# Attention and two feed-forward layers on one core: token blocks of 504 in place of 512, the first two of 472 and 504 in place of 384 and 512

## The chip, the cores and the metric

The kernel runs on one core of a Trainium2 chip. The metric is the device time of one execution in microseconds (us). The profile names the engines: PE is TensorE's matmul, PEld its weight loads, DVE is VectorE, ACT is ScalarE, POOL is GpSimd and SP is SyncE, which issues nearly all DMAs here.

## The reference

What is computed, for 6016 tokens of 256 channels in fp32:

```
qn = q / (norm(q over tokens) + 1e-6);  kn likewise          # q, k: 6016 x 256
a  = softmax(kn.T @ qn / tau)                                # 256 x 256
x  = v @ a                                                   # 6016 x 256
xn = x / rms(x over channels) * rms_g
y  = (silu(xn @ w_gate) * (xn @ w_val)) @ w_out              # d_ff 1536
h  = y @ w_in;  out = (h - tanh(h)) @ w_out2                 # d_ff 2048
```

The first layer's norm is per token; everything after the attention matrix `a` is a chain of matrix products over the tokens.

## The kernel before

Channels lie on the 128 partitions (two halves of 128) and tokens along the free axis, in blocks of up to 512, the width of one fp32 bank of PSUM. A product of 128 x 128 weights with n tokens is made as three fp32r matmuls of n columns each (`prod`, L440 to L453: high by high, low by high, high by low parts), so all weights and operands are split into a high part (a copy on ACT, `hi_of`) and a low part (a subtraction on DVE, `lo_of`). Every matmul has a weight load of its own. A few small or early products are plain fp32 matmuls (`matmul`, L455): the attention scores, `x` of the first two blocks, and the two matmuls of a norm. Each of those stands as two instructions in the trace.

The tokens are cut into twelve blocks, six pairs. Before, they are 384 and 512 for the first pair and 512 for the ten others. The stages are:

- The attention scores, then `x` of blocks 0 and 1 in fp32 (`x_full`), their norms by matmul (`x_post`: `ms` is the mean of squares, `narm`, `nary` and `nart` are the small tiles of the reciprocal root on DVE, `r` spreads it over 128 partitions), and meanwhile `x` of blocks 2 and 3 in three parts (`x_products`).
- The first layer for blocks 0 and 1 with ordinary products (`gate_block`): for each of 12 slices f of the hidden width 4 products (gate and value, two halves of channels) and 2 into the output sums `acc`, for each block: 72 products, so 216 matmuls of the block's width.
- The first layer for pairs 1 to 5 in the form of Strassen and Winograd (`unit`, `first_unit`), in which 7 products stand for 8 over the two blocks of a pair: 132 products a pair. The names in it are X, T, Y, Z with g for gate and v for value, and the operands B11, T1 to T4, B21, B22. Beside it run `x` and the norms of the next pair (`x_thread`): 7 products for each of pairs 2 to 5, and 8 for pair 1.
- The second layer for all six pairs in the same form (`second_unit`): 120 products a pair in 8 units of 7 products and 8 `acc` products. Its first pair takes the tokens of blocks 0 and 1 as two halves of equal width, 448 before.

No engine's order is written out by hand. The code builds a graph of operations (`Graph`), and a planner simulates the engines with cost formulas (`act_cost`, `dve_cost`, n/2.4 + 13.7 ns for a matmul) and emits each engine's instructions in the order found. `LAG1` is the distance, in the planner's time, at which the `acc` products of pairs 1 to 5 are ranked behind the other products of TensorE.

Of the kernel before, what the change touches and what calls it, by code (L numbers as in the profile page):

```python
# [16 lines left out]
P = 128  # L17
# [284 lines left out]
ROUNDS = 6  # L302
FIRST_PIECES, LAST_PIECES = [[1, 1, 2], [2, 2], [2, 2]], [2, 1]
# [3 lines left out]
LAG0, LAG1, LAG2 = 4100.0, 10000.0, 4800.0  # L307
# [4 lines left out]
def attn_moe_kernel(  # L312
# [621 lines left out]
    def x_post(b, xs, ms_tag, r_tag):  # L934

        n = blocks[b][1]
        NG = n // P
        T = {}

        def square(c):  # L940
            T[f"sq{c}"] = sq_tile(f"sq{c}_{b}")
            activation(T[f"sq{c}"][:, :n], xs[c][:, :n], AF.Square, n)

        def gain(c):
            T[f"xg{c}"] = ox(f"x{c}_{b}")
            activation(T[f"xg{c}"][:, :n], xs[c][:, :n], AF.Copy, n, scale=g_t[:, c:c + 1])

        def ms(key=None):
            sq = T["sq0"][:, :n]
            tt("add", sq, sq, T["sq1"][:, :n], n)  # L950
            T["o"] = bank(ms_tag, f"ms{b}")
            for t in range(NG):
                matmul(T["o"][:, 2 * t:2 * t + 2], T["sq0"][:, t * P:(t + 1) * P], mean32, P,
                       True, True, key=key)

        def rs():
            m, y, t = (narrow(x, f"b{b}") for x in "myt")
# [51 lines left out]
    def x_thread(p, take, out):  # L1009


        B = []
# [4 lines left out]
        def split_v(t):  # L1017
            raw = v_raw.pop(b0 + t)
            vh, vl = (new(wpool, f"gv{4 + t}{x}", f"v{x}{b0 + t}", V2, F32R) for x in "hl")
            for kk in range(KC):  # L1020
                g.op("ACT", act_cost(BLK), lambda kk=kk: nc.scalar.activation(
                    out=vh.t[:, kk], in_=raw.t[:, kk], func=AF.Copy), [raw], [vh.part(kk)])
            for kk in range(KC):
                dve(lambda kk=kk: nc.vector.tensor_sub(
                    out=vl.t[:, kk], in0=raw.t[:, kk], in1=f32(vh.t[:, kk])), BLK, 2,
                    [raw, vh.part(kk)], [vl.part(kk)])
            split[t] = vh, vl

        def x_out(t, c, o):
            sqs[t].append(sq_tile(f"sq{b0 + t}_{c}"))  # L1030
            activation(sqs[t][c], o, AF.Square, BLK)
            B.append(ox(f"x{b0 + t}_{c}g"))
            activation(B[-1], o, AF.Copy, BLK, scale=g_t[:, c:c + 1])

        def x_products(t):
            for c in range(KC):
                o = take(f"x{b0 + t}_{c}", c)
                for kk in range(KC):
                    vh, vl = split[t]
                    prod(o, a_hl[kk][c], tuple(  # L1040
                        x.view(lambda a, kk=kk: a[:, kk], kk) for x in (vh, vl)), BLK, kk == 0)
                x_out(t, c, o)

        def v_forms():
# [33 lines left out]
            tt("sub", t2, b21, t2, BLK)  # L1078
            tt("sub", b12, b22, b12, BLK)
# [4 lines left out]
        def x_unit():  # L1084
# [4 lines left out]
            def x_to(t, c):  # L1089
                def f(o, m5=None):  # L1090
                    sqs[t][c] = sq_tile(f"sq{b0 + t}_{c}")
                    x = B[KC * t + c] = ox(f"x{b0 + t}_{c}g")
                    if m5 is not None:
                        add(x, o, m5, BLK)
                    elif (t, c) == (0, 1):
                        copy(x, o, BLK)
                    else:
                        activation(sqs[t][c], o, AF.Square, BLK)
                        copy(x, o, BLK)
                        return  # L1100
                    activation(sqs[t][c], x, AF.Square, BLK)
# [13 lines left out]
        def turn_blocks(e, across):  # L1115
            dve(lambda: nc.vector.transpose(out=across.t, in_=e.t), BLK, 2, [e], [across])
# [71 lines left out]
        yield from operands(B, BLK, out)
# [293 lines left out]
    for p in range(1, NP):  # L1482
# [8 lines left out]
        A = Accumulate(out1_weight, NF1, [BLK, BLK], to_y(p), LAG1,  # L1491
                       rr if p + 1 < NP else sq_tile)
        for i in range(NU1):
# [3 lines left out]
            first_unit(i, x, BLK, A, between)  # L1497
# [60 lines left out]
```

## Time and profile before

| | |
|---|---|
| median of 3 runs | 1109.0 us (1108.97 to 1109.12) |
| profiled execution, its own time | 1108.96 us |
| its span in the trace | 1107.2 us |
| busy share: PE, PEld, DVE, ACT | 99%, 83%, 77%, 63% |
| granted clock of TensorE | 1.0 in every slice (2.4 GHz) |

The span runs from the first instruction to the last in the trace, and 1.8 us of the execution's time lie outside it. Matmuls overlap in the trace, since the end of one is modelled some 160 ns behind the start of the next; what one costs is the distance from its start to the start of the next, called its pitch below.

### The profile page before, as it was taken

The numbers are of one execution on the slowest core, as the hardware profiler recorded it, in microseconds if no ns is written. First come the engines' busy times: TensorE is split into PE (matmuls) and PEld (weight loads), VectorE is DVE, ScalarE is ACT, GpSimd is POOL, SyncE is SP. The second block draws the span as 40 slices with busy tenths as digits, with TensorE's granted clock in tenths as the row PEclk, the third lists the DMA queues.
The fourth block names the chain that finished last, engine by engine and source line by source line (L and its number), as shares of the span: only waits on it lengthen the run. The fifth ranks groups of instructions, "written<-read, shape, count | busy, mean of one in ns | idle before, by whom it ended". The sixth has DMA issues, their size and how long they took to land.

```text
span 1107.2 us, 14156 instructions
## 1 busy us (share of the span) xinstructions
PE 1101.4 (99%) x4944; PEld 921.4 (83%) x4944; DVE 852.2 (77%) x1473; ACT 696.0 (63%) x1223; POOL 0.7 (0%) x6
## 2 busy tenths in 40 slices
PE   9999999999999999999999999999999999999998
PEld 8798988888888888888888899888888888888886
DVE  6999897887788788778766967768668668667664
ACT  7776466666566556646566766657656656656664
POOL 0000000000000000000000000000000000000000
PEclk9999999999999999999999999999999999999999
DMA  9952121114212211311322201101101101100101
GB/s 352 388 196 96 58 72 58 39 38 143 77 39 76 68 58 46 122 58 54 120 81 66 89 1 29 44 1 38 39 1 39 38 1 29 39 1 1 39 1 38
DMA packets 41480, 76.75 MB, mean 69 GB/s; under 512 B 5313, under 2 KB 10945, under 8 KB 41409
## 3 DMA queue, kind: packets, MB, share of 16 engines
q1 hardware_dynamic: 40976, 75.47, 20.4%
q8 instruction: 38, 0.62, 0.2%
q10 hardware_dynamic: 432, 0.39, 0.1%
q14 instruction: 34, 0.27, 0.1%
HBM read 54.00 MB, written 21.78 MB: 68 GB/s over the span
## 4 chain that ended last, share of the span: by engine, by line
PE 98%; DVE 1%; DMA 0%; ACT 0%; SPq 0%; issue 0%; DVEq 0%; ACTq 0%
PE acc L451 40%; PE Yh L451 9%; PE Xh L451 6%; PE Yv L451 6%; PE Yg L451 5%; PE Xg L451 4%; PE Xv L451 4%; PE S L459 4%; PE Zh L451 3%; PE Th L451 3%; PE g L451 3%; PE v L451 3%; PE Zv L451 2%; PE Tg L451 2%; PE Zg L451 2%; PE Tv L451 2%
## 5 line engine op out<-in xcount | busy, mean ns | idle before, releaser
L432 DVE TENSOR_TENSOR ulc<-wc,uc 128x512 fp32r<-128x512 f32 (+1 forms) x192 | 130.2, 679 | 83.7 <-ACT uc L413 81.4
L413 ACT ACTIVATE uc<-wc 128x512 fp32r<-128x512 f32 (+1 forms) x192 | 119.3, 623 | 99.7 <-PE acc L451 86.9
L413 ACT ACTIVATE uc<-tc 128x512 fp32r<-128x512 f32 x120 | 73.3, 627 | 86.5 <-DVE tc L428 82.9
L432 DVE TENSOR_TENSOR ulc<-tc,uc 128x512 fp32r<-128x512 f32 x120 | 79.4, 683 | 0.7 <-ACT uc L413 0.4
L428 DVE TENSOR_TENSOR Zv<-Yv,m5v 128x512 f32<-128x512 f32 x30 | 20.9, 698 | 42.8 <-PE Yv L451 40.7
L413 ACT ACTIVATE wc<-Xh 128x512 f32<-128x512 f32 (+1 forms) x48 | 28.2, 588 | 30.5 <-PE Xh L451 30.5
L428 DVE TENSOR_TENSOR wc<-Xh,wc 128x512 f32<-128x512 f32 (+1 forms) x48 | 32.6, 678 | 19.1 <-ACT wc L413 19.0
L428 DVE TENSOR_TENSOR Zh<-Yh,m5h 128x512 f32<-128x512 f32 (+1 forms) x48 | 33.0, 687 | 16.9 <-ACT m5h L413 14.8
L459 PE MATMUL S<-q,k 128*128 128x256 f32 x188 | 42.2, 384 | 0.5 <-DMA k<-k_in 0.5
L459 PEld LDWEIGHTS S<-q,k 128*128 128x128 f32 x188 | 35.8, 193 | 5.6 <-DMA q<-q_in 0.9
L428 DVE TENSOR_TENSOR wc<-Yh,wc 128x512 f32<-128x512 f32 (+1 forms) x48 | 32.6, 679 | 9.4 <-ACT wc L413 9.3
L413 ACT ACTIVATE wc<-Yh 128x512 f32<-128x512 f32 (+1 forms) x48 | 28.1, 586 | 14.8 <-PE Yh L451 14.8
L428 DVE TENSOR_TENSOR acc<-acc,sq 128x512 f32<-128x512 f32 (+1 forms) x46 | 29.5, 678 | 8.4 <-ACT sq L413 7.7
L413 ACT ACTIVATE m5h<-Th 128x512 f32<-128x512 f32 (+1 forms) x48 | 28.2, 588 | 11.3 <-PE Th L451 11.3
L413 ACT ACTIVATE Yh<-Xh 128x512 f32<-128x512 f32 (+1 forms) x48 | 27.6, 575 | 11.6 <-PE Xh L451 10.4
L428 DVE TENSOR_TENSOR wc<-s,wc 128x512 f32<-128x512 f32 (+1 forms) x48 | 32.3, 674 | 0.8 <-ACT wc L413 0.8
L413 ACT ACTIVATE r<-acc 128x512 f32<-128x512 f32 (+3 forms) x49 | 27.1, 579 | 9.1 <-PE acc L451 8.6
L428 DVE TENSOR_TENSOR wc<-Zh,wc 128x512 f32<-128x512 f32 (+1 forms) x48 | 32.3, 673 | 0.7 <-ACT wc L413 0.7
L428 DVE TENSOR_TENSOR s<-Yh,m5h 128x512 f32<-128x512 f32 (+1 forms) x48 | 32.5, 677 | 0.1
L413 ACT ACTIVATE tc<-Xg 128x512 f32<-128x512 f32 x30 | 17.9, 596 | 22.9 <-PE Xg L451 22.8
L451 PE MATMUL acc<-ulc,w12h 128*128 128x512 f32 x80 | 31.2, 390 | 0.0
L451 PE MATMUL acc<-uc,w12l 128*128 128x512 f32 x80 | 31.2, 390 | 0.0
(984 smaller groups left out, 3489.3 us busy)
## 6 DMA issues: line engine op xcount, KB each, us to landing
vraw<-vT_in SPq DMA_DIRECT2D x11, 512.0 KB, 4.3
y<-r SPq DMA_DIRECT2D x22, 256.0 KB, 2.0
y<-y SPq DMA_DIRECT2D x20, 256.0 KB, 2.6
outT<-r SPq DMA_DIRECT2D x19, 256.0 KB, 2.1
q<-q_in SPq DMA_DIRECT2D x8, 512.0 KB, 9.5
k<-k_in SPq DMA_DIRECT2D x8, 512.0 KB, 9.3
raw<-w_in_in SPq DMA_DIRECT2D x8, 512.0 KB, 4.3
l<-y SPq DMA_DIRECT2D x16, 256.0 KB, 2.9
```

The costliest lines, as they stand in the source:

```text
L413: nc.scalar.activation(out=ap(out), in_=ap(in_), func=func, **{x: ap(a) for x, a in kw.items()})
L428: return dve(lambda: f(out=ap(out), in0=ap(a), in1=ap(b)), n, 2, [a, b], [out])
L432: lambda: nc.vector.tensor_sub(out=ap(out), in0=ap(in_), in1=f32(ap(hi))), n, 2,
L451: nc.tensor.matmul(o, ap(a), ap(b), start=start and i == 0, stop=i == 2, skip_group_check=True)
L459: lambda: nc.tensor.matmul(ap(out), ap(a), ap(b), start=start, stop=stop, **kw),
```

## The change

A constant `SIZE = 504` takes the place of the block width 512 in the token split, with REST = 6016 mod 1008 = 976. Blocks are then 472 and 504 for the first pair and 504 for the ten others, and the two halves of the first pair in the second layer are 488 wide in place of 448. Tiles keep their 512 columns, and operations take the first 504 of them. 504, 472 and 488 are no multiples of 128 or 32, so the norms handle a rest: in `x_post` the last group of 128 tokens starts at n - 128 and overlaps the one before it (block 0 has four groups in place of three); in `x_thread` the turning of 32 x 32 blocks is a piece of 480 columns and one of 32 that overlaps it, and the load of the norms is one of 480 columns and one of 24. `LAG1` goes from 10000 to 11500.

```diff
+SIZE = 504
-LAG0, LAG1, LAG2 = 4100.0, 10000.0, 4800.0
+LAG0, LAG1, LAG2 = 4100.0, 11500.0, 4800.0
...
-    REST = N % (2 * BLK) or 2 * BLK
-    blocks = [(0, REST - min(BLK, REST)), (REST - min(BLK, REST), min(BLK, REST))]
-    blocks += [(t, BLK) for t in range(REST, N, BLK)]
+    REST = N % (2 * SIZE) or 2 * SIZE
+    blocks = [(0, REST - min(SIZE, REST)), (REST - min(SIZE, REST), min(SIZE, REST))]
+    blocks += [(t, SIZE) for t in range(REST, N, SIZE)]
...
-        NG = n // P
+        starts = [t * P for t in range(n // P)] + ([n - P] if n % P else [])
+        NG = len(starts)
...
-            for t in range(NG):
-                matmul(T["o"][:, 2 * t:2 * t + 2], T["sq0"][:, t * P:(t + 1) * P], mean32, P,
+            for t, at in enumerate(starts):
+                matmul(T["o"][:, 2 * t:2 * t + 2], T["sq0"][:, at:at + P], mean32, P,
                        True, True, key=key)
...
         def turn_blocks(e, across):
-            dve(lambda: nc.vector.transpose(out=across.t, in_=e.t), BLK, 2, [e], [across])
+            whole = n // G * G
+            cols = [(0, 0, whole)] + ([(whole, n - G, G)] if n % G else [])
+            for to, at, size in cols:
+                dve(lambda to=to, at=at, size=size: nc.vector.transpose(
+                    out=across.t[:, to:to + size], in_=ap(e)[:, at:at + size]), size, 2, [e], [across.part(to)])
+            across.part().w = [w for to, _, _ in cols for w in across.part(to).w]
...
-            dma(rs[t], back.view(lambda a, t=t: a[t:t + 1, :].to_broadcast([P, BLK])), BLK * P * 4,
-                [back], [rs[t]])
+            whole = n // G * G
+            cols = [(0, 0, whole)] + ([(whole, whole + G - n % G, n % G)] if n % G else [])
+            for to, at, size in cols:
+                dma(rs[t].view(lambda a, to=to, size=size: a[:, to:to + size], to),
+                    back.view(lambda a, t=t, at=at, size=size:
+                              a[t:t + 1, at:at + size].to_broadcast([P, size])), size * P * 4,
+                    [back], [rs[t].part(to)])
...
-        n = REST // 2 if p == 0 else BLK
+        n = REST // 2 if p == 0 else SIZE
...
-        A = Accumulate(out1_weight, NF1, [BLK, BLK], to_y(p), LAG1,
+        A = Accumulate(out1_weight, NF1, [SIZE, SIZE], to_y(p), LAG1,
```

The remaining lines of the diff put n or SIZE where BLK stood. Since the planner sees other costs, the order of instructions moves. The second layer's order on TensorE stays as it was but for the widths; the first layer's and the start's do not. Lines of the changed kernel are one higher than before (L459 becomes L460).

On TensorE at the start, around `x_full` (vraw are the values v, a the attention matrix, vh and vl the parts of v of block 2, ms the mean of squares of block 0), before:

```order
L459 MATMUL x_1_513<-vraw_371,a_486 128x512
L459 MATMUL x_0_492<-vraw_367,a_518 128x384
L459 MATMUL x_1_499<-vraw_367,a_518 128x384
L459 MATMUL x_0_505<-vraw_371,a_518 128x512
L459 MATMUL x_1_513<-vraw_371,a_518 128x512
L451 MATMUL x_0_552<-vh_468,ah_490 128x512
L451 MATMUL x_0_552<-vh_468,al_501 128x512
L451 MATMUL x_0_552<-vl_476,ah_490 128x512
L459 MATMUL ms_561<-mean_81,sq_0_540 128x2 x3
```

and in the changed kernel:

```order
L460 MATMUL x_1_514<-vraw_371,a_486 128x504
L452 MATMUL x_0_528<-vh_468,ah_490 128x504
L452 MATMUL x_0_528<-vh_468,al_499 128x504
L452 MATMUL x_0_528<-vl_476,ah_490 128x504
L460 MATMUL x_0_492<-vraw_367,a_524 128x472
L460 MATMUL x_1_501<-vraw_367,a_524 128x472
L460 MATMUL x_0_508<-vraw_371,a_524 128x504
L460 MATMUL x_1_514<-vraw_371,a_524 128x504
L452 MATMUL x_0_528<-vh_468,ah_538 128x504
L452 MATMUL x_0_528<-vh_468,al_543 128x504
L452 MATMUL x_0_528<-vl_476,ah_538 128x504
L460 MATMUL ms_570<-mean_81,sq_0_541 128x2 x4
```

Three matmuls of block 2 moved ahead of the second half of `x_full`. Between `ms` and the spreading matmul `r` of block 0 there are then 9 of these matmuls, where there were 12.

On DVE a little later, the reciprocal root of block 0's norm, for which `r` waits (it begins with narmb from ms and ends with the last naryb; w10, gv1 and a are other work), before, from its third instruction on:

```order
L428 TENSOR_TENSOR a_518<-a_518,a_486 128x128
L472 SCALAR_TENSOR_TENSOR nartb_588<-naryb_579,narmb_574 128x6
L428 TENSOR_TENSOR a_486<-a_518 128x128
L475 TENSOR_TENSOR nartb_588<-nartb_588,naryb_579 128x6
L476 SCALAR_TENSOR_TENSOR nartb_588<-nartb_588 128x6
L632 TENSOR_TENSOR w10l<-w10y,w10h 128x512
L479 SCALAR_TENSOR_TENSOR naryb_579<-nartb_588,naryb_579 128x6
L482 SCALAR_TENSOR_TENSOR nartb_588<-naryb_579,narmb_574 128x6
L958 TENSOR_SCALAR narmb_610<-ms_594 128x8
L485 TENSOR_TENSOR nartb_588<-nartb_588,naryb_579 128x6
L558 TENSOR_SCALAR gv1y<-gv1y 128x512
L488 SCALAR_TENSOR_TENSOR naryb_579<-nartb_588,naryb_579 128x6
```

and in the changed kernel, the whole of it:

```order
L960 TENSOR_SCALAR narmb_586<-ms_570 128x8
L470 TENSOR_SCALAR naryb_588<-narmb_586 128x8
L473 SCALAR_TENSOR_TENSOR nartb_592<-naryb_588,narmb_586 128x8
L476 TENSOR_TENSOR nartb_592<-nartb_592,naryb_588 128x8
L477 SCALAR_TENSOR_TENSOR nartb_592<-nartb_592 128x8
L480 SCALAR_TENSOR_TENSOR naryb_588<-nartb_592,naryb_588 128x8
L559 TENSOR_SCALAR gv1y<-gv1y 128x512
L483 SCALAR_TENSOR_TENSOR nartb_592<-naryb_588,narmb_586 128x8
L559 TENSOR_SCALAR gv1y<-gv1y 128x512
L486 TENSOR_TENSOR nartb_592<-nartb_592,naryb_588 128x8
L960 TENSOR_SCALAR narmb_614<-ms_594 128x8
L489 SCALAR_TENSOR_TENSOR naryb_588<-nartb_592,naryb_588 128x8
```

The three operations on `a` and the subtraction for w10 no longer stand inside this chain; one operation on gv1 more does.

On TensorE in the first layer, in the last unit of pair 2, around its gate products (uc and ulc are the parts of a finished slice of the hidden width), before:

```order
L451 MATMUL Tg_3188<-T1h,sh_1987 128x512
L451 MATMUL Tg_3188<-T1h,sl_2057 128x512
L451 MATMUL Tg_3188<-T1l,sh_1987 128x512
L451 MATMUL acc_2653<-uc_3158,w12h 128x512
L451 MATMUL acc_2653<-uc_3158,w12l 128x512
L451 MATMUL acc_2653<-ulc_3166,w12h 128x512
L451 MATMUL Yg_3186<-T2h,sh_1987 128x512
L451 MATMUL Yg_3186<-T2h,sl_2057 128x512
L451 MATMUL Yg_3186<-T2l,sh_1987 128x512
L451 MATMUL Xg_3162<-B21h,gv5h 128x512
L451 MATMUL Xg_3162<-B21h,gv5l 128x512
L451 MATMUL Xg_3162<-B21l,gv5h 128x512
```

and in the changed kernel:

```order
L452 MATMUL Yg_3210<-T2h,sh_1864 128x504
L452 MATMUL Yg_3210<-T2h,sl_1967 128x504
L452 MATMUL Yg_3210<-T2l,sh_1864 128x504
L452 MATMUL Xg_3182<-B21h,gv5h 128x504
L452 MATMUL Xg_3182<-B21h,gv5l 128x504
L452 MATMUL Xg_3182<-B21l,gv5h 128x504
L452 MATMUL acc_2690<-uc_3178,w12h 128x504
L452 MATMUL acc_2690<-uc_3178,w12l 128x504
L452 MATMUL acc_2690<-ulc_3186,w12h 128x504
```

The first `acc` product of the slices with the weights w12 moved from ahead of Yg's product with T2 to behind Xg's with B21, two products later.

## Rows read from the trace of the kernel before

**Rows 1.** The page's first part: span; busy time, share and instructions of each engine.

```profile
span 1107.2 us, 14156 instructions
PE 1101.4 (99%) x4944; PEld 921.4 (83%) x4944; DVE 852.2 (77%) x1473; ACT 696.0 (63%) x1223; POOL 0.7 (0%) x6
```

**Rows 2.** The chain that ended last, by engine.

```profile
PE 98%; DVE 1%; DMA 0%; ACT 0%; SPq 0%; issue 0%; DVEq 0%; ACTq 0%
```

**Rows 3.** What PE waited for: total us, times, longest us.

```profile
PE nrm L459 <- DVE mean L506: 1.1, 1, 1.1
PE S L459 <- DMA k<-k_in: 0.5, 1, 0.5
PE Yv L451 <- DVE Zv L428: 0.2, 1, 0.2
```

**Rows 4.** Busy time by stretch: from:to, length, each engine's busy us (count), clock, DMA.

```profile
50.00:75.00 25.00, 24.88 (x127) 20.71 (x126) 24.27 (x66) 23.25 (x46) 0.00 (x0) 1.00 0.68 236
75.00:100.00 25.00, 25.00 (x126) 22.61 (x126) 24.84 (x40) 14.65 (x25) 0.00 (x0) 1.00 0.42 147
142.87:613.74 470.87, 470.65 (x2068) 387.04 (x2068) 374.18 (x667) 290.79 (x517) 0.00 (x0) 1.00 0.23 72
651.54:660.84 9.30, 9.30 (x46) 8.45 (x45) 6.50 (x12) 5.38 (x11) 0.00 (x0) 1.00 0.00 0
708.50:718.70 10.20, 10.20 (x46) 8.45 (x45) 6.72 (x11) 5.91 (x11) 0.00 (x0) 1.00 0.00 0
```

**Rows 5.** Timeline, PE, first layer of blocks 0 and 1: start us, us, instruction.

```profile
99.32 0.39 PE L451 MATMUL g<-xh,gv2h 128*128 128x512 f32 x1
...
105.03 0.33 PE L451 MATMUL acc<-u,w11h 128*128 128x384 f32 x1
...
106.59 0.39 PE L451 MATMUL g<-xh,gv2h 128*128 128x512 f32 x1
```

**Rows 6.** Timeline, PE, second layer, pair 0: first matmuls of two units that follow.

```profile
651.55 0.37 PE L451 MATMUL Xh<-B11h,l24h 128*128 128x448 f32 x1
...
660.85 0.37 PE L451 MATMUL Xh<-B11h,l25h 128*128 128x448 f32 x1
```

**Rows 7.** The same in pair 1.

```profile
708.52 0.39 PE L451 MATMUL Xh<-B11h,l22h 128*128 128x512 f32 x1
...
718.72 0.39 PE L451 MATMUL Xh<-B11h,l23h 128*128 128x512 f32 x1
```

**Rows 8.** Timeline, PE, the start: `x_full` and what follows it.

```profile
48.03 6.18 PE L459 MATMUL x<-vraw,a 128*128 128x384 f32 x16
...
54.27 0.40 PE L451 MATMUL x<-vh,al 128*128 128x512 f32 x1
```

**Rows 9.** Timeline, PE, norm matmuls of block 1 (ms) and block 0 (r), and their followers.

```profile
56.80 0.95 PE L459 MATMUL ms<-mean,sq 128*128 128x2 f32 x8
57.60 0.49 PE L451 MATMUL x<-vh,ah 128*128 128x512 f32 x1
...
59.09 0.90 PE L459 MATMUL r<-ident,naryb 128*128 128x128 f32 x6
59.74 0.48 PE L451 MATMUL x<-vh,ah 128*128 128x512 f32 x1
```

**Rows 10.** Timeline, DVE and PEld, reciprocal root of block 0's norm, first and last.

```profile
55.82 0.16 DVE L958 TENSOR_SCALAR narmb<-ms 128x6 f32<-128x6 f32 x1
...
58.84 0.16 DVE L488 SCALAR_TENSOR_TENSOR naryb<-nartb,naryb 128x6 f32<-128x6 f32 x1
...
59.05 0.30 PEld L459 LDWEIGHTS r<-ident,naryb 128*128 128x128 f32 x2 [0.23 <-DVE naryb L488]
```

**Rows 11.** DVE groups and DMA issues of the later norms: count, busy us, mean ns; KB, us.

```profile
L1116 DVE STREAM_TRANSPOSE across<-sq 128x512 f32<-128x512 f32 x10 | 6.8, 694 | 0.0
rs<-back SPq DMA_DIRECT2D x10, 256.0 KB, 3.6
```

**Rows 12.** Timeline, PE, last matmul.

```profile
1102.84 0.39 PE L451 MATMUL acc<-ulc,l27h 128*128 128x512 f32 x1
```

More of the change, by code (lines that the diff above doesn't have):

```diff
@@ L964, in spread @@
             T["y"] = bank(r_tag, f"r{b}")
-            for t in range(NG):
-                matmul(T["y"][:, t * P:(t + 1) * P],
+            for t, at in enumerate(starts):
+                matmul(T["y"][:, at:at + P],
                        T["yn"].view(lambda a, t=t: a[:, 2 * t:2 * t + 1].to_broadcast([P, P])),
@@ L1020, in split_v @@
             for kk in range(KC):
-                g.op("ACT", act_cost(BLK), lambda kk=kk: nc.scalar.activation(
-                    out=vh.t[:, kk], in_=raw.t[:, kk], func=AF.Copy), [raw], [vh.part(kk)])
+                g.op("ACT", act_cost(n), lambda kk=kk: nc.scalar.activation(
+                    out=vh.t[:, kk, :n], in_=raw.t[:, kk, :n], func=AF.Copy), [raw], [vh.part(kk)])
             for kk in range(KC):
                 dve(lambda kk=kk: nc.vector.tensor_sub(
-                    out=vl.t[:, kk], in0=raw.t[:, kk], in1=f32(vh.t[:, kk])), BLK, 2,
+                    out=vl.t[:, kk, :n], in0=raw.t[:, kk, :n], in1=f32(vh.t[:, kk, :n])), n, 2,
                     [raw, vh.part(kk)], [vl.part(kk)])
@@ L1176, in x_thread @@
             rs.append(sq_tile(f"rs{p}_{t}"))
-            dma(rs[t], back.view(lambda a, t=t: a[t:t + 1, :].to_broadcast([P, BLK])), BLK * P * 4,
-                [back], [rs[t]])
+            whole = n // G * G
[5 more added lines that the diff above has]
+                    [back], [rs[t].part(to)])
+            rs[t].part().w = [w for to, _, _ in cols for w in rs[t].part(to).w]
         for t in range(2):
             for c in range(KC):
-                x = B[KC * t + c]
+                x, r = B[KC * t + c][:, :n], rs[t][:, :n]
                 if p == 1:
-                    tt("mul", x, x, rs[t], BLK)
+                    tt("mul", x, x, r, n)
                 else:
-                    dve(lambda x=x, r=rs[t], c=c: nc.vector.scalar_tensor_tensor(
+                    dve(lambda x=x, r=r, c=c: nc.vector.scalar_tensor_tensor(
                         out=ap(x), in0=ap(x), scalar=ap(g_t[:, c:c + 1]), in1=ap(r), op0=ALU.mult,
-                        op1=ALU.mult), BLK, 2, [x, rs[t], g_t], [x])
-        yield from operands(B, BLK, out)
+                        op1=ALU.mult), n, 2, [x, r, g_t], [x])
+        yield from operands(B, n, out)
     y_dram = [new_dram(f"y{b}", [C, n]) for b, (_, n) in enumerate(blocks)]
     def y_thread(p, out):
-        n = REST // 2 if p == 0 else BLK
+        n = REST // 2 if p == 0 else SIZE
         B = []
@@ L1201, in y_thread @@
                     src = y_dram[2 * p + t]
-                    dma(b, src.view(lambda a, rows=rows: a[rows, :], kk), P * BLK * 4, [src.part(kk)], [b])
+                    dma(b[:, :n], src.view(lambda a, rows=rows: a[rows, :], kk), P * n * 4,
+                        [src.part(kk)], [b])
                     continue
@@ L1496, in between @@
                     next(thread)
-            first_unit(i, x, BLK, A, between)
+            first_unit(i, x, SIZE, A, between)
             if p + 1 < NP:
@@ L1510, in attn_moe_kernel @@
         x, x_next = x_next, {}
-        n = REST // 2 if p == 0 else BLK
+        n = REST // 2 if p == 0 else SIZE
         thread = y_thread(p + 1, x_next) if p + 1 < NP else iter(())
```

53 lines of the change are left out of this document (27 added, 26 removed).

## Prediction

> **What bounds the kernel now.** I read four views. The page's first part shows PE busy for 1101.4 of 1107.2 us, with DVE at 77% and ACT at 63% [rows 1]. The chain that ended last lies on PE for 98% of the span [rows 2], and PE's waits on other engines come to 1.8 us in all [rows 3]. So the question is what TensorE's 4944 instructions cost, not what they wait for. The busy share by stretch confirms it and shows the one place where another engine is as full: from 50 to 100 us DVE is busy 24.27 and 24.84 of each 25 us [rows 4]. The clock is 1.00, the 2.4 GHz level, in all these stretches.
>
> The timeline gives the pitch of one fp32r matmul. In the second layer a unit is 15 products, 45 matmuls, and the load engine counts 45 in the stretch of one unit [rows 4]. With 512 columns a unit takes 718.72 - 708.52 = 10.20 us [rows 7], 226.7 ns each; 512 columns at 2.4 GHz are 213.3 ns, so 13.3 ns come on top. With 448 columns a unit takes 660.85 - 651.55 = 9.30 us [rows 6], 206.7 ns each, where the columns are 186.7: 20.0 ns on top. With 384, nine matmuls take 106.59 - 105.03 = 1.56 us [rows 5], 173.3 ns, 13.3 on top again. So 384 and 512 carry the same surplus of 32 cycles, and 448 carries 48. The whole forecast hangs on where 504, 488 and 472 fall, since one nanosecond on 4680 matmuls is 4.7 us.
>
> **The change, part by part.**
>
> *Columns.* The number of fp32r matmuls stays: by the loops 216 of block 0's width in the first layer, 360 of pair 0's half width in the second, and 4104 of full width (216 of block 1, 24 and 84 for x, 5 x 396 and 5 x 360 in the two layers). Before, that is 216 x 384 + 360 x 448 + 4104 x 512 = 2,345,472 columns; after, 216 x 472 + 360 x 488 + 4104 x 504 = 2,346,048. The 80 tokens that join the first pair lose the saving of 7 products for 8 in the first layer, but need fewer columns elsewhere. The balance is 576 columns, +0.24 us.
>
> *Surplus per matmul.* Taken at 13.3 ns for 504 and 472, it changes nothing. For 488 I take 13.3 as well, so the 360 matmuls of pair 0 lose 6.7 ns each: -2.4 us. Why 13.3: all three new widths are nearer to 512 in the one respect that the rows let me think of as a cause. In each stretch one weight load goes with one matmul, and 45 loads take 8.45 us [rows 4], 188 ns each. 448 columns stream in 186.7 ns, just about as long as such a load; 512 take longer, 384 are well shorter, and both carry the small surplus. 472, 488 and 504 columns (196.7, 203.3 and 210 ns) lie on the side of 512. That is an argument from two lengths, not a measurement. The bounds for 504 are 20.0 ns from above (+27.4 us over 4104 matmuls) and, from below, the fp32 matmuls: 16 of `x_full` and one fp32r product take 54.27 - 48.03 = 6.24 us [rows 8]; less 0.23 that is 6.01 us for 8 x (384 + 512) columns in two passes, 5.97 us at 2.4 GHz, hence 2.5 ns of surplus each. If 504 had that, 4104 matmuls would save 44 us. I see nothing that would do so and use a small part of it below.
>
> The Trainium skill bears on this term: its page "TensorE: Matmul & The Clock Gate", section "Back-to-back issue gap", gives the warm spacing as N/2.4 + 2.5 ns, a fixed cost whatever the width. The fp32 matmuls here agree with its 2.5; the fp32r ones, at 13.3 and 20.0, do not. By that rule the 448 columns would owe nothing extra, the -2.4 would fall away, and the forecast would be 1110.2 us.
>
> *x_full.* Eight instructions grow from 384 to 472 columns and eight shrink from 512 to 504: +640 columns. At 6.01 us for 7168 [rows 8] that is +0.54 us.
>
> *Norm matmuls of the first blocks.* Block 0 has four groups for three: two more instructions for ms, at 0.80 us for 8 [rows 9], and two more for r, at 0.65 us for 6: +0.20 and +0.22.
>
> *Hidden parts.* The 32-column turns are ten more DVE instructions; ten of 512 columns cost 694 ns each [rows 11], so each new one is below that, and DVE has 97 of 471 us free in this stage [rows 4]. The ten DMAs of 24 columns wait on the same norms as the ten of 480, which take 3.6 us to land [rows 11]; the chain has the rest of a pair's 94 us (470.87 / 5) to finish. If that cover were gone, one pair would be late by some 4 us. Element-wise work has the same number of instructions and the same tokens. The last copy and store shrink by 8 columns: nothing that counts, after the last matmul at 1102.84 [rows 12].
>
> *Order at the start.* r of block 0 waits for DVE's reciprocal root, which runs from 55.82 to 59.00 us, and r's load did wait 0.23 us for it [rows 10]. Four operations leave this chain (three of about 0.3 us on a, one of 0.7) and one of 0.4 joins, so it should take about 2 us, with the 0.5 us from the end of ms ahead of it 2.5. Ahead of r, PE now has 9 matmuls of 223 ns and ms of block 1, 0.8 us: 2.8 us. It fits, barely, and I set it at zero; behind r stand the products of blocks 0 and 1, for which nothing else could fill in.
>
> *LAG1.* Later acc products lengthen no chain as long as other products fill the place. The first layer's pairs lose little now: 2068 matmuls in 470.87 us [rows 4] are 2.1 us above 226.7 ns each. That is all that a better order could win there.
>
> Sum: 0.24 - 2.4 + 0.54 + 0.42 = -1.2 us. The span of 1107.2 becomes 1106.0; with the 1.8 us outside it, 1107.8, which stands as well against the median, 1109.0, since the profiled execution took 1108.96.
>
> **The rivals.**
>
> *A: 504 carries the 20 ns of 448* (slower). Its mechanism would be that only widths of whole 128 columns have the small surplus; 384 and 512 are such, 448 is not, and neither are the new ones. For it: it describes all three rows. Against it: one odd width only. 4104 x 6.67 ns is 27.4 us, 216 of 472 columns add 1.4, and 488 keeps its 20 ns: 1109.0 + 1.2 + 28.8 = 1139 us. It turns the result to slower from a surplus of 14 ns on.
>
> *B: the pitch goes in steps.* 416, 496 and 544 cycles are all multiples of 16. If 504 + 32 is rounded up to 544, the full-width matmuls win nothing from being shorter: 4104 x 3.33 ns = +13.7, the other two widths +1.9: 1107.8 + 15.6 = 1123 us. Against it: the three widths are multiples of 16 themselves, so they cannot tell, and the fp32 rows show no such step.
>
> *C: what 448 pays is not won back at 488, while 504 has 13.3 ns.* The cause of the 6.7 ns would then not be that a weight load takes as long as the columns. For it: nothing shows the cause; against it: 488 is nearer to 512 than to 448. The -2.4 falls away: 1110.2 us. The rule of the Trainium skill's page "TensorE: Matmul & The Clock Gate" named above would give this time too.
>
> *D: waits from the new order.* If r of block 0 or the first gate product of block 1 waits in the stretch where DVE is full, 1 to 3 us are lost; if norms come late in one pair, 4. Some 1111.5 us.
>
> *E: the order is better.* Of the 2.1 us lost in the first layer and the 0.07 us at each change of width in blocks 0 and 1 (18 matmuls of each width take 106.59 - 99.32 = 7.27 us [rows 5] where the pitches give 7.20, twelve times), half goes away: 1.5 us, hence 1106.3.
>
> *F: 504 has a smaller surplus than 512*, by the 8 cycles of B in the other direction: 4680 x 3.33 = -15.6 us, 1092.
>
> **How the numbers follow.** Chances: the forecast 0.50, with 1106.3 to 1109.5 as its own range; A 0.07, B 0.06, C 0.10, D 0.08, E 0.11, F 0.08. 0.2% of the time, 2.2 us, is about what a measurement can tell from no change. Faster by more than that, below 1106.8, are E, F and a third of the forecast's half, since its sum is only 1.0 us from that bound: 0.11 + 0.08 + 0.17 = 0.36. Slower, above 1111.2, are A, B and most of D: 0.20. The rest, 0.44, is the same. The range leaves out A, B and most of F, 0.19, and takes in the norms that come late: 1104 to 1112.5.
>
> **What would show it.** In the profile after, the distance between the first matmuls of two units in the second layer, divided by 45: 223.3 ns for 504 and 216.7 for 488 in the forecast, 230.0 in A, 226.7 in B, 220.0 in F. The nine matmuls of 472 columns should take 210 ns each. PE's waits should stay below 3 us; a wait of r for naryb, or of Yv or Yg for DVE, would be D. The sixteen instructions of x_full should take 0.5 us more. The prediction is wrong if the pitch at 504 is off 223.3 by more than 0.5 ns, before anything else.

## The result and the profile after

The changed kernel took 1122.75 us (median of four runs, 1121.52 to 1124.6) against 1109.06 us before: 1.0124 times as long, with a 95% interval of 1.0106 to 1.0141. It is slower by 13.7 us where 1.2 less were forecast, and far outside the range. Its runs lie 3 us apart, those of the kernel before half a microsecond. The profiled execution is the longest of the four, 1124.6 us with a span of 1121.4, so that 3.2 us of it lie outside the span, where the kernel before has 1.8; what follows compares spans. Three executions of kernels below, one with a first pair of 448 columns and two with 502, took at least 2.5% longer than the others of the same kernel and are left out of the medians.

The page of the changed kernel, first part, and the chain that ended last by engine:

```profile
span 1121.4 us, 14196 instructions
PE 1115.6 (99%) x4948; PEld 925.8 (83%) x4948; DVE 852.6 (76%) x1483; ACT 697.6 (62%) x1223; POOL 0.7 (0%) x6
...
PE 99%; ACT 0%; DVE 0%; issue 0%
```

PE's busy time rose by 14.2 us [rows 1] and the span by the same 14.2. DVE gained 0.4 us in its ten more instructions and ACT 1.6. The chain still lies on PE [rows 2]. What PE waited for (engine and line, total us, times, longest us):

```profile
PE nrm L460 <- DVE mean L507: 1.1, 1, 1.1
PE Yv L452 <- ACT Yv L414: 0.6, 1, 0.6
PE Yv L452 <- DVE Zv L429: 0.2, 1, 0.2
```

That is 1.9 us in all against 1.8 before [rows 3]. One wait is new, 0.6 us of Yv for ACT, at 186 us in the first layer's pair 1; one of 0.5 us for a load of k is gone. So the sum of the waits does not grow; the instructions themselves cost more. The windows of the changed kernel (from:to, length, busy us and count of PE, PEld, DVE, ACT and POOL, clock, DMA share, GB/s) show the first layer's pairs, one unit of the second layer's pair 0, and one of pair 1:

```profile
156.23:621.06 464.83, 463.96 (x2044) 383.21 (x2043) 360.12 (x654) 283.17 (x505) 0.00 (x0) 1.00 0.23 72
662.05:672.21 10.16, 10.16 (x46) 8.50 (x45) 6.49 (x11) 5.72 (x11) 0.00 (x0) 1.00 0.00 1
753.55:763.75 10.20, 10.20 (x47) 8.45 (x46) 6.65 (x11) 5.85 (x11) 0.00 (x0) 1.00 0.00 0
```

The last row decides about the prediction. A unit of 45 matmuls with 504 columns takes 10.20 us, 226.7 ns each, exactly what 45 with 512 columns took [rows 7]. The eight columns less save nothing. The middle row gives 488 columns 10.16 / 45 = 225.8 ns, almost as much as 504, where 448 took 206.7 [rows 6]. The clock is 1.00, the 2.4 GHz level, in all three. The timeline of PE (start us, us, instruction) shows where the two units begin and end, and in the stage of blocks 0 and 1 nine matmuls of 472 columns followed by eighteen of 504:

```profile
102.55 0.38 PE L452 MATMUL acc<-u,w11h 128*128 128x472 f32 x1
...
104.47 0.39 PE L452 MATMUL g<-xh,gv2h 128*128 128x504 f32 x1
...
108.55 0.38 PE L452 MATMUL g<-xh,gv3h 128*128 128x472 f32 x1
...
662.05 0.38 PE L452 MATMUL Xh<-B11h,l24h 128*128 128x488 f32 x1
...
672.21 0.39 PE L452 MATMUL Xh<-B11h,l25h 128*128 128x488 f32 x1
...
753.55 0.39 PE L452 MATMUL Xh<-B11h,l25h 128*128 128x504 f32 x1
...
763.75 0.39 PE L452 MATMUL Xh<-B11h,l26h 128*128 128x504 f32 x1
```

Nine of 472 take 104.47 - 102.55 = 1.92 us, 213.3 ns each (210 were forecast). Eighteen of 504 take 4.08 us, 226.7 ns here too. Counted in cycles of 2.4 GHz: 472 columns cost 512 cycles, 504 cost 544 like 512 columns, and 488 cost 542 in this unit.

Cut at the first matmul of each stage in the two traces (start, `x_full`, the first `g`, the first `Xg`, the first `Xh` of pair 1, the last matmul), the span divides so, in us:

| stage | before | after | difference |
|---|---|---|---|
| up to `x_full` | 48.03 | 48.00 | -0.03 |
| `x_full`, norms, x of blocks 2 and 3 | 13.87 | 14.75 | +0.88 |
| first layer, blocks 0 and 1 | 85.78 | 93.49 | +7.71 |
| first layer, pairs 1 to 5, and second layer, pair 0 | 541.07 | 546.45 | +5.38 |
| second layer, pairs 1 to 5 | 414.09 | 414.48 | +0.39 |
| behind the last matmul's start | 4.33 | 4.25 | -0.08 |

Nearly all of the loss lies where the columns per matmul grew (384 to 472, 448 to 488). Where 504 stand in place of 512, in some 415 us of the second layer, nothing was won. The 80 tokens that went into the first pair therefore cost their full price and were paid for nowhere. The order of the second layer's matmuls is the same before and after in pairs 1 to 5; in pair 0, 84 of the 360 stand at another place in it.

### The profile page after: what moved, and what is told of

The parts are those of the page before. It is cut to its first block, busy times and chain, and to the rows that moved or that the text cites. A ratio compares the mean times of both kernels' runs of the same rounds, so it can differ in the third digit from the quotient of the medians.

```text
span 1121.4 us, 14196 instructions
## 1 busy us (share of the span) xinstructions
PE 1115.6 (99%) x4948; PEld 925.8 (83%) x4948; DVE 852.6 (76%) x1483; ACT 697.6 (62%) x1223; POOL 0.7 (0%) x6
## 4 chain that ended last, share of the span: by engine, by line
PE 99%; ACT 0%; DVE 0%; issue 0%
PE acc L452 41%; PE Yh L452 9%; PE Xh L452 6%; PE Yg L452 5%; PE Yv L452 5%; PE S L460 4%; PE Xg L452 4%; PE Xv L452 4%; PE Zh L452 3%; PE Th L452 3%; PE v L452 3%; PE g L452 3%; PE Zv L452 2%; PE Tv L452 2%; PE Tg L452 2%; PE Zg L452 2%
## 5 line engine op out<-in xcount | busy, mean ns | idle before, releaser
L433 DVE TENSOR_TENSOR ulc<-wc,uc 128x504 fp32r<-128x504 f32 (+1 forms) x192 | 130.2, 679 | 84.4 <-ACT uc L414 83.6
L414 ACT ACTIVATE uc<-wc 128x504 fp32r<-128x504 f32 (+1 forms) x192 | 119.6, 624 | 103.0 <-PE acc L452 91.0
L414 ACT ACTIVATE uc<-tc 128x504 fp32r<-128x504 f32 x120 | 73.0, 621 | 68.2 <-DVE tc L429 57.9
L433 DVE TENSOR_TENSOR ulc<-tc,uc 128x504 fp32r<-128x504 f32 x120 | 79.1, 675 | 2.9 <-PE acc L452 1.8
L429 DVE TENSOR_TENSOR wc<-Xh,wc 128x504 f32<-128x504 f32 (+1 forms) x48 | 32.6, 678 | 19.7 <-ACT wc L414 19.6
L429 DVE TENSOR_TENSOR Zh<-Yh,m5h 128x504 f32<-128x504 f32 (+1 forms) x48 | 33.0, 688 | 17.9 <-ACT m5h L414 15.2
L460 PE MATMUL S<-q,k 128*128 128x256 f32 x188 | 42.7, 387 | 0.1
L429 DVE TENSOR_TENSOR wc<-Yh,wc 128x504 f32<-128x504 f32 (+1 forms) x48 | 32.6, 679 | 12.3 <-ACT wc L414 12.3
L460 PEld LDWEIGHTS S<-q,k 128*128 128x128 f32 x188 | 36.0, 194 | 5.5 <-issue 0.7
L429 DVE TENSOR_TENSOR wc<-s,wc 128x504 f32<-128x504 f32 (+1 forms) x48 | 32.3, 674 | 0.9 <-ACT wc L414 0.8
L429 DVE TENSOR_TENSOR wc<-Zh,wc 128x504 f32<-128x504 f32 (+1 forms) x48 | 32.3, 672 | 0.7 <-ACT wc L414 0.7
L429 DVE TENSOR_TENSOR s<-Yh,m5h 128x504 f32<-128x504 f32 (+1 forms) x48 | 32.5, 678 | 0.2
```

The costliest lines, as they stand in the source:

```text
L414: nc.scalar.activation(out=ap(out), in_=ap(in_), func=func, **{x: ap(a) for x, a in kw.items()})
L429: return dve(lambda: f(out=ap(out), in0=ap(a), in1=ap(b)), n, 2, [a, b], [out])
L433: lambda: nc.vector.tensor_sub(out=ap(out), in0=ap(in_), in1=f32(ap(hi))), n, 2,
L460: lambda: nc.tensor.matmul(ap(out), ap(a), ap(b), start=start, stop=stop, **kw),
```

## The experiments

### The pitch by itself

The first question was whether the width alone does this. Streams of 64 equal fp32r matmuls in a kernel that holds nothing else, with widths from 512 down to 384, then one with 64 columns of weights and one in bf16:

```
for n in range(512, 376, -8):
    run(w, x, n)                 # 64 matmuls, four PSUM banks, four weights in turn
```

> The disputed cost by itself: the reference is left out; 64 fp32r matmuls at each of 22 widths, each with its own weight load, four banks in turn, no other engine at work; then 504 columns that start at column 8, then weights of 64 columns, then bf16. Theory 1 (the pitch goes in steps: width + 32 cycles, rounded up to a step of 16): 512, 504, 496, 488, 480, 472 cycles wide give 544, 544, 528, 528, 512, 512 cycles, that is 226.7, 226.7, 220.0, 220.0, 213.3, 213.3 ns; 448 gives 480 cycles, 200.0 ns, and 384 gives 416, 173.3 ns. Theory 2 (the surplus comes from ACT, DVE and DMA at the same memory): without them every width has the same small surplus, 504 at or below 223.3 ns and 448 at or below 200.0. Theory 3 (only whole 128 columns have the small surplus): 512 and 384 at 13.3 ns on top, all others at 20.0, 504 at 230.0. If the surplus belongs to the weight load, weights of 64 columns halve it.

Windows of this kernel over 64 matmuls each, with 512, 504, 496, 488, 480, 472, 448 and 416 columns, then 504 and 448 with 64 columns of weights, and 504 in bf16:

```profile
22.17:36.68 14.51, 14.51 (x65) 12.02 (x64) 0.00 (x0) 0.00 (x0) 0.00 (x0) 1.00 0.00 1
36.68:51.19 14.51, 14.51 (x65) 12.01 (x64) 0.00 (x0) 0.00 (x0) 0.00 (x0) 1.00 0.00 0
51.19:65.49 14.30, 14.30 (x66) 12.01 (x64) 0.00 (x0) 0.00 (x0) 0.00 (x0) 1.00 0.00 1
65.49:79.56 14.07, 14.07 (x65) 12.01 (x64) 0.00 (x0) 0.00 (x0) 0.00 (x0) 1.00 0.00 0
79.56:93.43 13.87, 13.87 (x65) 12.01 (x64) 0.00 (x0) 0.00 (x0) 0.00 (x0) 1.00 0.01 1
93.43:107.08 13.65, 13.65 (x65) 11.97 (x64) 0.00 (x0) 0.00 (x0) 0.00 (x0) 1.00 0.00 0
133.80:147.02 13.22, 13.22 (x65) 12.02 (x64) 0.00 (x0) 0.00 (x0) 0.00 (x0) 1.00 0.00 1
184.52:196.47 11.95, 11.95 (x65) 11.93 (x65) 0.00 (x0) 0.00 (x0) 0.00 (x0) 1.00 0.01 1
...
331.11:345.85 14.74, 14.74 (x65) 8.64 (x64) 0.00 (x0) 0.00 (x0) 0.00 (x0) 1.00 0.00 1
359.88:372.83 12.95, 12.95 (x66) 8.43 (x64) 0.00 (x0) 0.00 (x0) 0.00 (x0) 1.00 0.00 1
386.65:400.25 13.60, 13.60 (x65) 6.26 (x64) 0.00 (x0) 0.00 (x0) 0.00 (x0) 1.00 0.00 1
```

Each length of the first eight divided by 64 gives 226.7, 226.7, 223.4, 219.8, 216.7, 213.3, 206.6 and 186.7 ns, in cycles 544, 544, 536, 528, 520, 512, 496 and 448. So 504 costs what 512 costs with DVE, ACT and DMA at rest. The steps in this stream are not those of rival B: by its multiples of 16, 496, 480 and 448 would stand at 528, 512 and 480. Nor does it go by whole 128 columns, as in rival A: 416 columns carry 32 cycles on top, as 512 do, and 504 carry 40 and not the 48 of 448. The weight load, on whose length I had rested the 13.3 ns, is not the cause of what 504 pays either: with 64 columns of weights it takes 8.64 / 64 = 135 ns in place of 188, and the pitch at 504 is 230.3 ns, not lower. The pitch at 448 is then 12.95 / 64 = 202.3 ns in place of 206.6, but streams further down show 448 at 202.7 with full loads too. In bf16 the same 504 columns take 212.5 ns, 2.5 above the columns. The rule of the Trainium skill's page "TensorE: Matmul & The Clock Gate", section "Back-to-back issue gap" (N/2.4 + 2.5 ns, which the section gives for an isolated matmul), agrees with that row, and not with the fp32r rows above it.

### The same with the kernel's order and with other engines at work

The kernel's three matmuls of a product (high, low, high parts) in place of four weights in turn, first beside ACT and DVE working without a pause, then alone:

```
for i in range(150): nc.scalar.activation(out=ta[i % 2], in_=raw[:, :512], func=AF.Copy)
for i in range(130): nc.vector.tensor_sub(out=td[i % 2], in0=raw[:, :512], in1=raw[:, 512:])
for n in (512, 504, 488, 448): three(n)      # 96 matmuls each
...
for n in (512, 504, 488, 448): three(n)
```

> Matmuls alone again, the reference left out: the kernel's pattern of three into one bank (two weight tiles, two moving tiles), first beside busy ACT and DVE, then quiet, at 512, 504, 488 and 448; then six more widths; then runs of 18 of 384 and 512 in turn, and of 472 and 504. If other engines make the surplus of 488 in the kernel (224.6 ns against 220.0 alone), it is about 224.6 beside them and 220.0 quiet; if the pattern makes it, both have 224.6. 512 and 504 stay at 226.7 in both. Between 504 and 512 the step is at the last columns: 506 and 510 still carry about 40 cycles, 510 above 226.7 ns. 436 and 444 carry about 40 cycles, 428 about 32. Turns of 384 and 512 lose 0.07 us per pair of runs, as in the kernel.

Windows of this kernel, 96 matmuls each: 504 beside the busy engines and alone, 488 beside them and alone; then, from its end, eighteen of 384 and eighteen of 512, and eighteen of 472 and eighteen of 504:

```profile
30.42:52.19 21.77, 21.77 (x98) 18.03 (x97) 21.77 (x37) 21.77 (x43) 0.00 (x0) 1.00 0.00 0
135.39:157.15 21.76, 21.76 (x97) 18.02 (x96) 0.00 (x0) 0.00 (x0) 0.00 (x0) 1.00 0.00 0
52.19:73.31 21.12, 21.12 (x98) 18.02 (x97) 21.12 (x36) 21.12 (x42) 0.00 (x0) 1.00 0.00 1
157.15:178.27 21.12, 21.12 (x97) 18.02 (x96) 0.00 (x0) 0.00 (x0) 0.00 (x0) 1.00 0.00 1
...
293.58:300.85 7.27, 7.27 (x37) 6.52 (x36) 0.00 (x0) 0.00 (x0) 0.00 (x0) 1.00 0.01 2
330.57:338.49 7.92, 7.92 (x38) 6.76 (x37) 0.00 (x0) 0.00 (x0) 0.00 (x0) 1.00 0.00 0
```

The pitches are 226.7 and 220.0 ns, whether DVE and ACT are busy for the whole window or idle. Busy engines don't make the surplus, and neither does the pattern of three. But 488 is at 220.0 ns here and at 225.8 in the changed kernel, which is taken up below. A change of width costs something as well: eighteen of 384 and eighteen of 512 in turn take 7.27 us where their pitches give 7.20, as in the kernel before [rows 5], while eighteen of 472 and eighteen of 504 take 7.92, just what their pitches give. Of the widths between, 506 and 510 came at 226.7 and 227.1 ns and 436 and 444 at 197.8 and 200.0, some 40 cycles over their columns or a little less; 428, expected at 32 cycles over, came at 43 (196.1 ns).

### LAG1 taken back, and LAG1 alone

```diff
 # the changed kernel
-LAG0, LAG1, LAG2 = 4100.0, 11500.0, 4800.0
+LAG0, LAG1, LAG2 = 4100.0, 10000.0, 4800.0
 # the kernel before
-LAG0, LAG1, LAG2 = 4100.0, 10000.0, 4800.0
+LAG0, LAG1, LAG2 = 4100.0, 11500.0, 4800.0
```

> The changed kernel with LAG1 put back to 10000, widths as changed. If the loss comes from the widths (theories 1 and 3), the time stays within 1.5 us of the changed kernel's 1122.8. If the later acc products cost it, it goes back towards 1108.

> The kernel before with LAG1 = 11500 alone. In the changed kernel LAG1 = 11500 is worth 3 us against 10000. If that is a gain of the order itself, the kernel before has at most the 2.1 us that its first layer's pairs lose now: 1107 to 1108. If the gain only mends waits that the new widths brought, it stays at 1109.0, or gets slower.

With the old LAG1 the changed kernel takes 1125.88 us, 1.0151 of before (1.0135 to 1.0168). The new one is thus worth some 3 us to it, though the two intervals overlap by a little. In the traces it is 2.4 us: 548.11 against 546.45 us in the first layer's pairs and the second layer's pair 0, and 5.05 against 4.25 behind the last matmul's start. Of the first difference one wait is a part, which the trace with the old LAG1 has and that of the changed kernel has not:

```profile
PE Yg L452 <- ACT Yg L414: 0.7, 1, 0.7
```

That the 0.8 us at the very end come from LAG1, which ranks products of the first layer, is not shown. In the kernel before, the new LAG1 gives 1108.61 us, 0.9994 of its time (0.9985 to 1.0002): within what can be told from no change.

### 448 columns in another stage

Is the 20 ns of 448 its own, or that of the second layer's first pair? The changed code with blocks of 512 and a first pair of 448 and 448, LAG1 as before:

```diff
-SIZE = 504
+SIZE = 512
+    blocks[:2] = [(0, REST // 2), (REST // 2, REST // 2)]
```

> The changed kernel with SIZE = 512, LAG1 = 10000 and the first pair cut into 448 and 448 (before: 384 and 512): only the first pair's blocks differ from before. By the pitches measured alone (448 at 496 cycles, 384 at 416, 512 at 544) each of the 216 pairs of matmuls costs 992 cycles for 960, 2.9 us, and block 0's fourth norm group 0.4 us: 1112.3. If 448 is dear only in the second layer's first pair, because of what else runs there, it is 480 here as well, and the sum is 1109.0 + 0.4 + 0 = 1109.4.

It took 1113.37 us, 1.0038 of before (1.0023 to 1.0053), 1.1 above the 1112.3 that the pitches gave. PE's timeline of this kernel, first layer, blocks 0 and 1, nine matmuls of 448 columns apart:

```profile
72.56 0.37 PE L453 MATMUL v<-xh,gv0h 128*128 128x448 f32 x1
...
74.42 0.37 PE L453 MATMUL g<-xh,gv1h 128*128 128x448 f32 x1
```

1.86 / 9 = 206.7 ns, as in the second layer before [rows 6]. So the 20 ns are not bound to that stage. Twice 448 also costs more than 384 and 512 for the same 896 tokens: 2 x 206.7 = 413.4 ns against 173.3 + 226.7 = 400.0, and over 216 matmuls that is 2.9 us by the pitches; this stage takes 88.33 us in its trace, 2.55 more than before, of the 4.2 lost in all.

### Two columns less: 502

If the surplus goes by width, two columns less should bring a lower step within the real kernel, with blocks of 494 and 502 and halves of 498:

```diff
-SIZE = 504
+SIZE = 502
```

> The changed kernel with blocks of 494 and 502 tokens (halves of 498) in place of 472 and 504 (488). Theory 1 (a matmul costs a number of cycles that stays the same over eight widths, eight times the whole eights of its width and 40 more, as the uniform streams showed): 502 takes 536 cycles, 223.3 ns, 494 takes 528, 220.0 ns, and the halves of 498 take 536, 223.3 ns; over the 4,104 sets of two blocks and the 216 pairs of halves that is some 30,500 cycles under the changed kernel, 12.7 us, so 1110 us, as long as before. Theory 2 (40 cycles more than the width at any width from 440 up): 542, 534 and 538 cycles, so 502 at 225.8 ns, and the time stays that of the changed kernel, 1121 to 1123 us. Theory 3 (504 is dear for another reason that the kernel brings, and 502 shares it): above 1120 us with 226 ns or more for 502.

It took 1114.04 us (the profiled execution 1114.33), 1.0042 of before (1.0024 to 1.0059), 8.7 less than with 504. Windows of this kernel: one unit of pair 0 (498 columns), and one of pair 1 (502):

```profile
658.20:668.40 10.20, 10.20 (x46) 8.50 (x45) 6.88 (x11) 5.80 (x11) 0.00 (x0) 1.00 0.00 0
749.38:759.43 10.05, 10.05 (x46) 8.45 (x45) 6.62 (x11) 5.84 (x11) 0.00 (x0) 1.00 0.00 0
```

502 columns take 10.05 / 45 = 223.3 ns, 536 cycles: a step of eight cycles under 504, as theory 1 said. Theories 2 and 3, by which the time stays at 1120 us or more, fall. But 498 takes 226.7, more than 502 does, and 494, over the 216 matmuls of its stage, 223.3 on average, where the theory had 223.3 and 220.0. These two misses are 360 x 3.3 + 216 x 3.3 ns = 1.9 us of the 4.3 between 1110 and the 1114.33 of the profiled execution. Of the rest, the trace shows 1.35 us at the start, in `x_full`'s stage and behind the last matmul (+0.35, +0.45 and +0.55 against the changed kernel). With 502 the kernel is still slower than before, since 536 cycles for 502 columns are 1.068 a column and 544 for 512 are 1.0625.

### LAG1 further up in the kernel before

```diff
-LAG0, LAG1, LAG2 = 4100.0, 10000.0, 4800.0
+LAG0, LAG1, LAG2 = 4100.0, 13000.0, 4800.0
```

> The kernel before with LAG1 at 13000 in place of 10000; 11500 gave 1108.6. If the first layer's last contractions still wait for results at 11500, a further 0.3 to 1 us is won: 1107.6 to 1108.3. If nothing waits there any more, the time is that of 11500 or is longer, since the work that is put off lengthens the tail behind the last halves: 1108.6 to 1110.

It took 1108.28 us, 0.9990 of before (0.9981 to 0.9999): the best time of all that ran, by less than the 0.2% that can be told from no change, and not told apart from 1108.61. What little is won in the two traces with a later LAG1 is not won by a better order. In them the 448 columns of pair 0 run at 202.7 and 202.9 ns, where they ran at 206.2: over 330 matmuls that is 1.1 to 1.2 us, more than the 0.5 and 0.6 us by which the two spans are shorter.

### What runs ahead of a width

Two kernels of matmuls alone ask for the fine steps, and why 488 and 448 show two pitches. The first replays the order of widths of the second layer's pair 0, then runs uniform streams. The second puts sixty of each width behind thirty of 512, 504 and 384:

```
runs([(504, 6), (488, 3), (504, 21), (488, 3), (504, 12), (488, 9), ..., (504, 6), (488, 103)])
for n in (502, 498, 494, 486, 478, 470, 462, 454, 446, 512, 448, 384, 448, 504, 488, 512, 488): three(n)
# the second
for n in (506, 502, 500, 498, 496, 494, 490, 488, 486, 480, 472, 464, 456, 448):
    for ahead in (512, 504, 384): runs([(ahead, 30), (n, 60)])
```

> Matmuls alone, the reference left out: the widths in the order of the second layer's first pair of before (512 with 448) and of the changed kernel (504 with 488), then uniform streams of 502 down to 446. Theory 1 (eights): 502 and 498 at 536 cycles (223.3 ns), 494 at 528 (220.0), 486 at 520 (216.7), 478 at 512 (213.3), 470 at 504 (210.0), 462 at 496 (206.7), 454 and 446 at 488 and 480 (203.3 and 200.0). Theory 2 (width and 40): 225.8, 224.2, 222.5, 219.2, 215.8, 212.5, 209.2, 205.8 and 202.5 ns. For the pair's own 488, at 224.6 ns in the changed kernel and at 220.0 in a uniform stream: if the widths that run ahead of it decide, the replayed order shows 224 to 225 ns here too; if the kernel's other work does, it shows 220.

> Matmuls alone, the reference left out: sixty of each width from 506 down to 448, each behind thirty of 512, of 504 and of 384 columns. If the width alone sets the pitch, the three means of a width agree within half a nanosecond. If what ran ahead of it sets it too, 488 is 220.0 ns behind 504 and 225 to 226 behind 512, and 448 is 206 to 207 behind some and 202.7 behind others; then 502, which showed 223.3 to 223.6 ns in both programs so far, either holds behind all three (536 cycles are its own) or shows 226.7 behind 512.

Windows of the first: in the replayed order of before, twelve matmuls of 448 and the last 130; the last 103 matmuls of 488 in the replayed order of the changed kernel's pair 0; 96 of 502, 498 and 494; then 96 of 448 behind 512 and behind 384:

```profile
33.84:36.28 2.44, 2.44 (x14) 2.25 (x12) 0.00 (x0) 0.00 (x0) 0.00 (x0) 1.00 0.00 0
51.07:77.92 26.85, 26.85 (x131) 24.41 (x130) 0.00 (x0) 0.00 (x0) 0.00 (x0) 1.00 0.00 1
127.21:149.87 22.66, 22.66 (x104) 19.34 (x103) 0.00 (x0) 0.00 (x0) 0.00 (x0) 1.00 0.00 1
171.66:193.10 21.44, 21.44 (x98) 18.01 (x96) 0.00 (x0) 0.00 (x0) 0.00 (x0) 1.00 0.00 0
193.10:214.85 21.75, 21.75 (x97) 18.10 (x96) 0.00 (x0) 0.00 (x0) 0.00 (x0) 1.00 0.00 1
214.85:236.30 21.45, 21.45 (x98) 17.99 (x96) 0.00 (x0) 0.00 (x0) 0.00 (x0) 1.00 0.00 1
...
379.54:399.00 19.46, 19.46 (x98) 18.03 (x97) 0.00 (x0) 0.00 (x0) 0.00 (x0) 1.00 0.00 1
415.66:435.50 19.84, 19.84 (x98) 18.03 (x97) 0.00 (x0) 0.00 (x0) 0.00 (x0) 1.00 0.00 0
```

Windows of the second: 60 matmuls of 488 behind 512, 504 and 384:

```profile
451.34:464.88 13.54, 13.54 (x61) 11.34 (x60) 0.00 (x0) 0.00 (x0) 0.00 (x0) 1.00 0.00 0
471.69:484.89 13.20, 13.20 (x62) 11.27 (x60) 0.00 (x0) 0.00 (x0) 0.00 (x0) 1.00 0.01 1
490.09:503.64 13.55, 13.55 (x61) 11.35 (x61) 0.00 (x0) 0.00 (x0) 0.00 (x0) 1.00 0.01 1
```

The kernel's odd widths come back without the kernel: 502 takes 223.3 ns, 498 takes 226.6 and 494 takes 223.4. Theory 1 holds for three of its nine widths (502, 478, 446) and misses the others by eight cycles or, at 462, twelve; theory 2 comes within 0.7 ns of none. 502 holds 223.3 to 223.6 behind all three, and 504 stands at 226.7 to 227.3 in all of these streams.

Other widths have two pitches. In these windows 448 takes 202.7 ns behind 512 and 206.7 behind 384, and 488 takes 225.7, 220.0 and 225.8 behind 512, 504 and 384. So what ran ahead can decide between them, but the width directly ahead is not enough to tell which: in the replayed order of before, 448 stands behind 512 every time, runs at some 203 ns in its first five short runs, and at 26.85 / 130 = 206.5 in its last one, as it does in that kernel.

In the changed kernel's pair 0 both pitches of 488 stand side by side. Windows of it: one of the eight short runs, and the long run behind six matmuls of 504 (from 641.76 us on):

```profile
627.10:629.74 2.64, 2.64 (x14) 2.25 (x12) 2.62 (x6) 1.18 (x4) 0.00 (x0) 1.00 0.67 199
641.76:702.68 60.92, 60.92 (x271) 51.01 (x270) 43.42 (x70) 37.70 (x69) 0.00 (x0) 1.00 0.07 22
```

The short run takes 2.64 / 12 = 220.0 ns, the long one 60.92 / 270 = 225.6. In the slow stream of 488 in the matmuls alone the starts stand 227, 223, 224, 222, 221, 221 and 242 ns apart, over and over, give or take one; in the long run of pair 0 227, 223, 224, 221, 221, 222 and 242. It is the same rhythm. What starts it there is open: the replayed order, with the same widths, ran at 22.66 / 103 = 220.0 ns to its end.

## Why the prediction was wrong

**The step that failed** is the surplus per matmul, taken at 13.3 ns for 504 and 472 and at 13.3 for 488. It measured 226.7 - 210.0 = 16.7 ns at 504, 16.7 at 472, and at 488 a mean of 224.6 - 203.3 = 21.3 over the 327 matmuls of pair 0's stage. The cost: 4104 x 3.33 ns = 13.7 us, 216 x 3.33 = 0.7, and 360 x 7.9 = 2.9, together 17.3 above the forecast. That is more than the whole error in the span (14.2 + 1.2 = 15.4); what was won elsewhere is below. The argument from two lengths, 448 columns streaming as long as a weight load, fell too: with loads of 135 ns in place of 188 a matmul of 504 columns costs no less (230.3 ns), and with full loads 448 runs at 202.7 as well as at 206.7.

**Rival B** had the numbers, 226.7 ns at 504 and 1123 us, and a wrong reason: its multiples of 16 are not there at 480, and at 496 only behind 512. Its time is in part luck: it had 488 at 220.0 ns, which is 1.7 us too little over 360 matmuls, and 1.9 us were won elsewhere. A had put 504 at 230.0, F at 220.0. C's sign for 488 was right and its size too small, since 488 lost 1.3 ns more than the 20 of 448. I had named the step as the one on which the forecast hangs and yet put 0.06 on B, because two of the three rows allowed a constant and I took the constant. Three widths that are all multiples of 16 could not show a staircase.

**What held.** *Columns:* the counts stand. *`x_full`, norm matmuls, order at the start:* PE's timeline of the changed kernel shows it:

```profile
48.00 3.44 PE L460 MATMUL x<-vraw,a 128*128 128x472 f32 x8
...
55.46 0.39 PE L452 MATMUL x<-vh,al 128*128 128x504 f32 x1
...
59.80 1.05 PE L460 MATMUL r<-ident,naryb 128*128 128x128 f32 x8
60.61 0.47 PE L452 MATMUL x<-vh,ah 128*128 128x504 f32 x1
```

From 48.00 to 55.46 run the sixteen instructions of `x_full` and four fp32r ones: 7.46 - 0.91 = 6.55 us, 0.54 over the 6.01 of before, as forecast. The eight instructions of r start at 59.80, and the matmul behind them at 60.61, 0.81 us against 0.65 for six [rows 9]: +0.16 where 0.22 stood, and r waits for nothing. The stage as a whole took 0.88 us more; 0.54 + 0.42 = 0.96 was the sum. *Hidden parts:* no wait of PE names a transpose, a norm of the later pairs or one of the small DMAs. **D** came in small: not at r, but as the one new wait of Yv for ACT, 0.6 us.

**E's time came, beside the failed step, and only in part by its cause.** The stage of blocks 0 and 1 should cost 216 x (213.3 - 173.3) ns = 8.6 us more by the pitches and cost 7.7, so 0.9 us went away. That is not the order: it is the loss between widths, which 384 and 512 have and 472 and 504 have not, as the 7.27 and 7.92 us of the matmuls alone showed. The first layer's pairs and pair 0 should cost some 330 x 18.4 ns = 6.1 more, for the matmuls of pair 0 at 224.6 in place of 206.2, and cost 5.4: 0.7 less. Together they give back 1.6 us, about E's 1.5. Some 0.3 us more, about a tenth each, lie at the two ends of the span, in `x_full`'s stage and in the second layer's later pairs, and 17.3 - 1.2 - 1.9 make the 14.2 measured. The order had a part in the 0.7: with the old LAG1 the changed kernel's 2076 matmuls of 504 columns in these stages took 473.8 us against 473.0 for as many of 512 before, and with the new one 472.3. In the kernel before the new LAG1 won nothing of this kind: 473.5 us.

## What to carry to other kernels

Where one engine is full and its instructions are thousands of one shape, a change of the shape is a question of that shape's own price, so measure a stream of the new shape before reasoning about anything else. Two or three known points do not show a staircase between them, least of all when they are all multiples of the same number; the price per column (544 / 512 = 1.0625 cycles here, 1.079 at 504, 1.068 at 502, 1.083 at 384) tells at once which split of the tokens is cheap. A term that is only argued, on which the sum turns sign, deserves more chance for its rival than 0.06.

## What was not expected of the hardware

- In the streams above, without other work and at a clock of 1.00 (2.4 GHz), an fp32r matmul with its own weight load costs these cycles: 384 columns 416, 416 columns 448, 446 columns 480, 472 columns 512, 480 columns 520, 502 columns 536, 504 to 512 columns 544 (508 came at 546). Most of the steady pitches are multiples of eight cycles, but no one formula fits: 498 takes 544 and 502 takes 536, behind any of the three widths tried ahead of them.
- Some widths have two pitches and keep one through a long run: 448 (486 or 496 cycles), 488 (528 or 542), 496 (528 behind 512, 536 behind 504 and 384) and 500 (536, or 544 behind 384). In the kernel before, 448 ran at 206.2 ns on average in pair 0's stage; with LAG1 at 11500 or 13000 it ran at 202.7 and 202.9.
- The three widths of bf16 that ran lie 6 cycles over their columns: 510 cycles for 504, 494 for 488, 454 for 448.
- What inside TensorE makes the steps and the two pitches no run here shows.
